# Attention steps of a routed-attention and mixture-of-experts kernel, handed to the engines in another order

## The chip, the cores and the metric

The kernel runs on one core of a Trainium2 chip. The metric is the device time of one execution in microseconds (us). The kernel before took 677.1, 678.21 and 678.61 us in three runs, a median of 678.21.

The core has five instruction streams that matter here. PE (TensorE) does matrix products and transposes. DVE (VectorE), ACT (ScalarE) and POOL (GpSimd) work on whole tiles, and SP (SyncE) issues the DMAs. Each engine takes its own instructions strictly in the order in which they were written; between engines they wait for each other's results.

## What is computed

First comes an attention in which a query sees a key only if both have the same nearest centroid. Then every token goes to one of eight experts by a greedy pass over all logits, and each expert is two matrix products.

```python
q_assign = np.argmax(np.einsum('bhsd,hcd->bhsc', q_n, c_n), axis=-1)
k_assign = np.argmax(np.einsum('bhsd,hcd->bhsc', k_n, c_n), axis=-1)
mask = q_assign[:, :, :, None] == k_assign[:, :, None, :]
scores = scale * np.matmul(q, k.transpose(0, 1, 3, 2))
scores = np.where(mask, scores, -1000000000.0)
attn = np.exp(scores - np.max(scores, axis=-1, keepdims=True))
attn = attn / (np.sum(attn, axis=-1, keepdims=True) + 1e-09)
x = np.matmul(attn, v)                  # heads side by side: (3072, 512)
order = np.argsort(-(x @ w_gate).flatten())
# in that order: a token takes expert e if it has none yet and e has fewer than 384
h = np.maximum(x[mask] @ w1[e], 0.0)
out[mask] = h @ w2[e]
```

Shapes: 4 batches, 8 heads, 768 positions, 64 wide, 16 centroids for each head; 3072 tokens, 512 wide, 8 experts with 1024 hidden columns. All inputs are float32.

## The kernel before

**Tiling.** The attention is cut into 8 units u, each one batch and four heads. A unit has 24 key tiles of 128 keys, and each of them is a step s. float32 operands are split into a high and a low float16 part, which are multiplied separately.

**The steps.** One named step is one closure, mostly one instruction, or a few on one engine. Those that matter here, with their lines:

- `load` (L497) fetches q, k or v through SP's DMA queue, for unit 0 head by head (`load,0,k,2`). `loadc` (L518) fetches the centroids.
- `c0` (L528, DVE), `c1` (L531, ACT, a square root) and `c2` (L536, ten small DVE instructions) normalise the centroids; `c3` (L556, PE) transposes them and `c4` (L559, DVE) copies the result out.
- `split_sc` and `split_hi` (L648, L652, ACT or DVE) scale an operand and write its high part, `split_lo` (L657 on DVE, L659 on POOL) its low part. `dup` (L664, L666, ACT) copies the high part into a second operand.
- `ident` makes the identity matrix on POOL (two instructions in a library file, masks.py), which every PE transpose reads. `misc`, `wtio`, `zqb` and `zkb` are constant fills on POOL.
- `pt` (L746) transposes on PE, `ptc` (L750 on ACT, L752 on DVE) copies the transpose out. `trans` (L740) transposes by DMA instead, for units 1 to 7.
- `cent` and `cent0` (L671, PE) score against the centroids. `hot` and `hh` (L693 to L709) turn the scores into marks for the mask.
- `m_mm` (L788, PE) and `m_rd` (L792, DVE) find a bound of each row's scores. `row0`, `row1` (L806, L810, POOL), `rowt` and `row2` (L813, L817, DMAs from SP's queue) put these bounds into the query operand.
- `b_mm` (L827, L831, PE) makes the scores of a step, `b_exp` (L834, ACT) their exponentials, `res` (L842, POOL or DVE) the low part of these, `av` (L853 to L859, PE) multiplies with v.
- `et` (L571, ACT) is one tiny exponential without use of its own. It makes ACT load the table with the exponential there.
- `out0`, `out1`, `out2`, `hi0`, `hi1` (L863 to L889) divide by the row sums and split; `lg0`, `lg1`, `lg2` (L921 to L935) form the routing logits. For the last unit, `xpt` (L907, PE) and `xpc` (L750, L752) transpose on the core.
- `bb` and `bq` (L1045 to L1066, DVE) begin the routing. `bb,0,i` works on the first three batches, `bb,1,i` on the last; i=0 to 4 (L1045 to L1053) end in the one-hot matrix `oh`, i=5, 6, 8 and 10 (L1055 to L1059, L1066) make integer keys, and i=9 or `bq,x` (L1063) compares with digit offsets.
- `tab` is one of 86 small constants for the routing, nearly all on POOL.

**The order.** The whole attention is a text, `ATT_ORDER`, of 2004 such steps, under `tc.manual_schedule()`. A loop (L1082) reads it word by word and calls the closure of each; so the place of a word in the text sets where its instructions stand in the queues of their engines. The same text has the loads and the DMA transposes in it. After it a second text, `FFN_ORDER`, does the same for routing and experts; its first steps (`pkc`, `cnt`, `sat`, L1175, L1214, L1243) count digits with `oh`.

**The buffers.** Three PSUM banks hold score tiles (`psc`, "sc"), one the centroid scores and logits (`pmx`, "mx"), one the output (`av`). The exponentials lie in a ring of four pairs of steps.

Of the kernel before, what the change touches and what calls it, by code (L numbers as in the profile page):

```python
# [26 lines left out]
hh4,0,k zqb split_sc,0,k,3 load,0,v,- split_hi,0,k,1,P split_lo,0,k,1,P pt,0,ka,1 ptc,0,ka,1,D pt,0,qa,3 ptc,0,qa,3,D
pt,0,qa,2 split_hi,0,k,3,P split_lo,0,k,3,P split_hi,0,k,2,P pt,0,ka,3 split_sc,0,v,- split_hi,0,v,-,P zkb ptc,0,qa,2,D
hh5,0,k pt,0,kb,0 ptc,0,ka,3,D ptc,0,kb,0,D cent0,1,k cent0,1,q hh0,1 hh1,1 dup,0,q,0 hh5,0,q dup,0,k,3 pt,0,qb,0
split_lo,0,k,2,P pt,0,ka,2 hh2,1 dup,0,q,1 hh3,1 hh4,1,q dup,0,k,2 hh4,1,k ptc,0,qb,0,A m_mm,0,3 m_rd,0,3 m_mm,0,4  # L30
split_lo,0,v,-,P m_rd,0,4 ptc,0,ka,2,A m_mm,0,5 m_rd,0,5 hh5,1,q dup,0,k,1 load,1,v,- split_sc,1,v,- vs,0 vh2,0 vact,0 vl2,0
load,1,k,- split_sc,1,k,- tab,0 m_mm,0,2 m_rd,0,2 cent0,2,k cent0,2,q hh0,2 hh1,2 tab,31 hh2,2 pt,0,qb,1 ptc,0,qb,1,D
hh5,1,k tab,3 tab,2 hh3,2 hh4,2,k pt,0,kb,1 split_hi,1,k,-,P hh4,2,q zqm split_lo,1,k,-,P m_mm,0,0 m_rd,0,0 m_mm,0,1
m_rd,0,1 ptc,0,kb,1,A dup,0,q,3 hh5,2,k tab,30 dup,0,q,2 m_mm,0,7 load,1,q,- m_rd,0,7 split_sc,1,q,- pt,0,kb,2 ptc,0,kb,2,D
m_mm,0,11 m_rd,0,11 cent0,3,k cent0,3,q hh0,3 row1,0,0 row0,0,0 load,2,k,- pt,0,qm,0 hh5,2,q split_hi,1,q,-,P ptc,0,qm,0,A
trans,1,ka,- pt,0,qb,2 ptc,0,qb,2,A wd hh1,3 m_mm,0,8 m_rd,0,8 hh2,3 m_mm,0,6 m_rd,0,6 hh3,3 hh4,3,k et split_lo,1,q,-,P
trans,1,qa,- b_mm,0,1 b_exp,0,1 res,0,1,P b_mm,0,0 b_exp,0,0 res,0,0,P hh4,3,q hh5,3,k hh5,3,q m_mm,0,15 m_rd,0,15 m_mm,0,10
m_rd,0,10 m_mm,0,13 m_rd,0,13 tab,32 pt,0,kb,3 cent,1,k,0 cent,1,k,2 cent,1,k,1 ptc,0,kb,3,D split_hi,1,v,-,P
split_lo,1,v,-,P cent,1,k,3 hot0,1,k hot1,1,k load,2,q,- hot2,1,k hot3,1,k tab,7 pt,0,qb,3 ptc,0,qb,3,A b_mm,0,4 b_exp,0,4
tab,5 b_mm,0,3 m_mm,0,9 b_exp,0,3 res,0,4,P m_rd,0,9 row0,0,1 b_mm,0,5 b_exp,0,5 row1,0,1 hot4,1,k hot5,1,k m_mm,0,17  # L40
b_mm,0,2 b_exp,0,2 m_mm,0,16 res,0,2,P dup,1,k,- trans,1,kb,- m_rd,0,17 cent,1,q,0 split_hi,2,k,-,D m_rd,0,16 m_mm,0,20
m_rd,0,20 cent,1,q,3 cent,1,q,2 cent,1,q,1 hot0,1,q hot1,1,q pt,0,qm,1 ptc,0,qm,1,A m_mm,0,12 res,0,3,P m_rd,0,12 hot2,1,q
m_mm,0,14 res,0,5,P m_rd,0,14 av,0,0 av,0,1 av,0,2 dup,1,q,- row0,0,2 row1,0,2 b_mm,0,9 b_exp,0,9 hot3,1,q hot4,1,q hot5,1,q
trans,1,qb,- m_mm,0,19 m_rd,0,19 av,0,3 av,0,4 m_mm,0,22 m_rd,0,22 split_lo,2,k,-,D trans,2,ka,- load,2,v,- b_mm,0,10
b_exp,0,10 b_mm,0,7 b_exp,0,7 b_mm,0,6 b_exp,0,6 res,0,6,P m_mm,0,18 m_rd,0,18 av,0,5 out0,0,0 out1,0,0 out2,0,0,D tab,16
b_mm,0,8 b_exp,0,8 res,0,8,P pt,0,qm,2 m_mm,0,23 m_rd,0,23 ptc,0,qm,2,A hi0,0,0 hi1,0,0 vs,1 m_mm,0,21 b_mm,0,11 dup,2,k,-
# [1492 lines left out]
```

## Time and profile before

| | us |
|---|---|
| median of three runs | 678.21 (677.1 to 678.61) |
| the profiled execution, its own time | 678.19 |
| its span from the first to the last instruction | 676.4 |
| busy in it: PE | 637.9 |
| busy in it: POOL | 512.9 |
| busy in it: DVE | 498.5 |
| busy in it: ACT | 421.3 |

The attention fills the time up to about 371 us, the first routing round lies between there and about 400, and the experts with later routing rounds fill the rest. A busy share over the whole span is an average over these three. In a timeline a row gives the start, the busy time, the engine, the line, what is written and read, and in brackets how long the engine had been idle before, and what it waited for. PE's records overlap their successors, so that a busy PE is not a PE at its full rate. PEclk is the granted clock of TensorE as a share of 2.4 GHz: 1.00 is the higher of its two levels, 0.50 the lower one, 1.2 GHz.

### The profile page before, as it was taken

How to read it: one execution, taken by the hardware profiler on the slowest of the kernel's cores; microseconds unless marked ns; L12 is line 12 of the kernel's file. 1: busy time of each engine (PE TensorE's matmuls, PEld its weight loads, DVE VectorE, ACT ScalarE, POOL GpSimd, SP SyncE). 2: the span in 40 equal slices, each digit the busy share in tenths (PEclk: the TensorE clock that was granted, in tenths of full speed). 3: DMA queues.
4: the chain of work that ended last, by engine and by line, in shares of the span. 5: the costliest groups of instructions: out<-in, count | busy, mean ns of one | idle time of the engine just before them, and what ended most of it. 6: DMA issues, size and time to landing. Idle time of an engine off the chain costs nothing. (4 is left out here: it accounts for less than half of the span.)

```text
span 676.4 us, 19511 instructions
## 1 busy us (share of the span) xinstructions
PE 637.9 (94%) x8154; PEld 428.9 (63%) x8154; DVE 498.5 (74%) x1096; ACT 421.3 (62%) x560; POOL 512.9 (76%) x452
## 2 busy tenths in 40 slices
PE   4899999999999999999988479999999999999996
PEld 4567767777777777777767359554545454545453
DVE  5899999999988989986867777776858585832020
ACT  8987686766767575655554045859484757598221
POOL 8578889899999997999995055858594949498601
PEclk9799999999999999999999669999999999999998
DMA  7668978799959874933123063739576666696101
GB/s 239 140 144 199 210 156 214 144 149 206 207 115 177 196 143 100 167 73 74 29 51 72 25 234 108 267 105 286 182 209 226 179 222 168 240 302 206 47 1 47
DMA packets 175451, 105.85 MB, mean 156 GB/s; under 512 B 135426, under 2 KB 160002, under 8 KB 175362
## 3 DMA queue, kind: packets, MB, share of 16 engines
q1 hardware_dynamic: 171522, 92.01, 56.3%
q0 software_dynamic: 3840, 12.59, 5.0%
q8 instruction: 64, 1.05, 0.7%
q14 instruction: 25, 0.20, 0.1%
HBM read 58.77 MB, written 12.58 MB: 105 GB/s over the span
## 5 line engine op out<-in xcount | busy, mean ns | idle before, releaser
L842 POOL TENSOR_TENSOR rt<-pt 128x768 f16<-128x768 f32 x180 | 276.5, 1558 | 26.6 <-ACT pt L834 25.8
L834 ACT ACTIVATE pt<-sc 128x768 f32<-128x768 f32 x192 | 149.8, 811 | 93.9 <-PE sc L831 73.5
L792 DVE TENSOR_REDUCE mxs<-sc 128x1 f32<-128x768 f32 x192 | 176.1, 951 | 17.7 <-PE sc L788 17.2
L1457 PE MATMUL pf<-xgt,w1h 128*128 128x384 f16 (+1 forms) x640 | 130.2, 295 | 0.3 <-DVE xgt L752 0.2
L856 PE MATMUL av<-vh,rt 128*128 128x65 f16 x1152 | 120.6, 193 | 1.7 <-POOL rt L842 1.6
L853 PE MATMUL av<-vh,pt 128*128 128x65 f16 x1152 | 120.7, 194 | 1.1 <-DVE xb L889 1.1
L855 PE MATMUL av<-vl,pt 128*128 128x64 f16 x1152 | 120.4, 191 | 0.0
L855 PEld LDWEIGHTS <-pt 128*128 128x128 bf16 x1152 | 105.8, 98 | 8.6 <-issue 1.5
L853 PEld LDWEIGHTS <-pt 128*128 128x128 bf16 x1152 | 106.2, 97 | 7.3
L856 PEld LDWEIGHTS <-rt 128*128 128x128 f16 x1152 | 105.3, 97 | 1.9 <-POOL rt L842 1.9
L827 PE MATMUL sc<-qbt,kbt 99*128 99x384 f16 x384 | 94.4, 327 | 1.3 <-DVE mxs L792 0.7
L831 PE MATMUL sc<-qat,kat 128*128 128x384 f16 x384 | 94.4, 327 | 0.0
L788 PE MATMUL sc<-kbt,qbt 80*128 80x384 f16 x384 | 90.5, 330 | 2.2 <-DVE qbt L752 0.5
L1457 PE MATMUL pf<-xgt,w1l 128*128 128x384 f16 (+1 forms) x320 | 89.9, 295 | 0.0
L1415 ACT ACTIVATE wr<-wr 128x1024 f32<-128x1024 f32 x64 | 66.7, 1046 | 25.9 <-DMA wr<-in_moe_w_dram 25.3
L1457 PEld LDWEIGHTS <-w1h 128*128 128x128 f16 x640 | 58.0, 98 | 28.3 <-issue 0.9
L1499 PE MATMUL pf<-w2h,hh 128*128 128x512 f16 (+2 forms) x200 | 73.6, 370 | 0.0
L1499 PE MATMUL pf<-w2l,hh 128*128 128x512 f16 (+2 forms) x200 | 73.6, 370 | 0.0
L1499 PE MATMUL pf<-w2h,hl 128*128 128x512 f16 (+2 forms) x200 | 73.2, 370 | 0.0
L1425 POOL TENSOR_TENSOR w2l<-wr,w2h 128x1024 f16<-128x1024 f32 x32 | 67.6, 2133 | 7.3 <-ACT w2h L1418 6.8
L1425 POOL TENSOR_TENSOR w1l<-wr,w1h 128x1024 f16<-128x1024 f32 x32 | 67.4, 2133 | 1.5 <-ACT w1h L1418 1.3
L1489 DVE SCALAR_TENSOR_TENSOR hl<-pf,hh 128x384 f16<-128x384 f32 x56 | 30.9, 553 | 45.7 <-ACT hh L1486 40.2
(244 smaller groups left out, 1118.3 us busy)
## 6 DMA issues: line engine op xcount, KB each, us to landing
wr<-in_moe_w_dram SPq DMA_DIRECT2D x64, 512.0 KB
...
xg<-xrow,idx POOLq DMA_INDIRECT x24, 6.5
```

The costliest lines, as they stand in the source:

```text
L788: nc.tensor.matmul(p[:, half, :S // 2], QBT[u][:D + C, i, :], KBT[u][:D + C, h * J + half * 3:h * J + half * 3 + 3, :], start=True, stop=True)
L792: nc.vector.tensor_reduce(mxs[u % 3][:, i:i + 1], MP.pop((u, i))[:, :, :S // 2], axis=AX.XY, op=OP.max)
L827: nc.tensor.matmul(ps[:, half, :S // 2], KBT[u][:ER + 3, s, :], QBT[u][:ER + 3, cs, :], start=True, stop=False)
L831: nc.tensor.matmul(ps[:, half, :S // 2], KAT[u][:, s, :], QAT[u][:, cs, :], start=False, stop=True)
L834: nc.scalar.activation(pts[(u * 12 + s // 2) % RP][:, s % 2], MP.pop((u, "b", s))[:, :, :S // 2], AF.Exp, scale=ESC)
L842: (nc.vector if e == "D" else nc.gpsimd).tensor_sub(rts[x][:, s % 2], p.rearrange("p a b -> p (a b)"), hi_view(pts[x])[:, s % 2])
L853: nc.tensor.matmul(o[:, j, :D + 1], hi[:, js], VH[u][:, s, :D + 1], start=(kt == 0 and j == 0), stop=False, skip_group_check=True)
L855: nc.tensor.matmul(o[:, j, :D], hi[:, js], VL[u][:, s, :], start=False, stop=False, skip_group_check=True)
L856: nc.tensor.matmul(o[:, j, :D + 1], r[:, js], VH[u][:, s, :D + 1], start=False, stop=(kt == J - 1), skip_group_check=True)
L1425: nc.gpsimd.tensor_sub(lo, wrs[c], hi)
L1457: nc.tensor.matmul(o, (w1l if i == 2 else w1h)[x][:, c, fs], xgt[x][:, h + int(i == 1), ts], start=(first and i == 0), stop=(last and i == ...
L1499: nc.tensor.matmul(PS["o", p, g], (hl if i == 2 else hh)[x][:, f, g * P:(g + 1) * P], (w2l if i == 1 else w2h)[x][:, f, ds], start=(f == 0 ...
```

## The change

Only the text `ATT_ORDER` changes. It holds the same 2004 steps with the same arguments as before, permuted; nearly every place in it is another one. No closure, no buffer and no size changes, nor does `FFN_ORDER`. The first and the last lines of the text:

```diff
@@ first lines of ATT_ORDER @@
-misc wtio loadc c0 ident c1 c2,0 load,0,k,0 split_sc,0,k,0 c2,1 c2,2 c2,3 c2,4 c2,5 c2,6 split_hi,0,k,0,P load,0,q,0
-split_sc,0,q,0 split_hi,0,q,0,P split_lo,0,q,0,P pt,0,qa,0 c2,7 c2,8 c2,9 load,0,q,2 split_sc,0,q,2 split_hi,0,q,2,P c2,10
+load,0,k,0 split_sc,0,k,0 split_hi,0,k,0,P zkb wtio load,0,q,0 misc split_sc,0,q,0 wd load,0,q,1 loadc split_sc,0,q,1
+load,0,q,2 c0 load,0,k,2 c1 c2,0 c2,1 split_hi,0,q,0,P dup,0,q,0 c2,2 c2,3 c2,4 c2,5 c2,6 split_lo,0,k,0,P c2,7 c2,8 c2,9
+c2,10 load,0,q,3 load,0,k,1 split_sc,0,q,2 split_hi,0,q,2,P et split_lo,0,q,2,P ident pt,0,ka,0 ptc,0,ka,0,D
...
@@ last lines of ATT_ORDER @@
-hi1,7,3,1 bb,0,2 bb,0,3 xpt,0,0 xpt,0,1 xpc,0,A,0 xpt,1,0 xpt,1,1 xpc,0,A,1 xpc,1,D,0 xpc,1,D,1 lg0,7,1,0 lg0,7,1,1 bb,0,4
-tab,81 tab,82 tab,68 tab,71 lg1,7,1 lg2,7,1 xst,7,0 xst,7,1 bb,1,0 bb,1,9 bb,1,1 bb,1,2 bb,1,3 bb,1,4 bb,1,5 bb,1,6 bb,1,8
-bb,1,10 tab,18 tab,19 tab,58 tab,84 tab,63 tab,21 tab,53 tab,66
+out2,7,3,D,1 hi0,7,3,0 xpt,0,0 bb,0,6 hi0,7,3,1 xpt,0,1 xpc,0,A,0 lg1,7,0 lg2,7,0 hi1,7,3,0 xpt,1,0 hi1,7,3,1 xst,7,1 bq,1
+xpt,1,1 xpc,1,D,0 lg0,7,1,0 xpc,1,D,1 bq,2 xpc,0,A,1 lg0,7,1,1 lg1,7,1 bb,0,10 lg2,7,1 bb,1,0 bb,0,8 bb,1,1 bb,1,5 bb,1,9
+bb,1,2 bb,1,6 bb,1,3 bb,1,8 bb,1,10 bb,1,4 tab,42
```

ACT's queue from its start, before. `ss` is the centroids' sum of squares, `ld` a loaded operand, `ka` and `qa` the split operands of unit 0:

```order
L531 ACT_TABLE_LOAD
L531 ACTIVATE ss<-ss 128x1
L648 ACTIVATE ld_76<-ld_76 128x384
L652 ACTIVATE ka<-ld_76 128x6x64
L648 ACTIVATE ld_77<-ld_77 128x384
L652 ACTIVATE qa<-ld_77 128x6x64
```

And further down in ACT's queue before, its 42nd to 46th row (`pt` are exponentials, `etl` the output of `et`):

```order
L750 ACTIVATE qbt_119<-sc 3x768
L750 ACTIVATE qbt_119<-sc 128x768
L571 ACT_TABLE_LOAD
L571 ACTIVATE etl<-ss 128x1
L834 ACTIVATE pt_128<-sc 128x768 x2
```

ACT's queue from its start, after the change:

```order
L648 ACT_TABLE_LOAD
L648 ACTIVATE ld_76<-ld_76 128x384
L652 ACTIVATE ka<-ld_76 128x6x64
L648 ACTIVATE ld_77<-ld_77 128x384 x2
L531 ACT_TABLE_LOAD
L531 ACTIVATE ss<-ss 128x1
L652 ACTIVATE qa<-ld_77 128x6x64
L664 ACTIVATE qb<-qa 128x6x64
L648 ACTIVATE ld_77<-ld_77 128x384
L652 ACTIVATE qa<-ld_77 128x6x64
L571 ACT_TABLE_LOAD
L571 ACTIVATE etl<-ss 128x1
```

The square root stands behind the first splits, and a table load of its own stands before it. The load for the exponential stands at the eleventh place, where it stood before at the 44th. ACT has three table loads where it had two.

POOL's queue around the identity, before (`vm` and `rest` are fills, `wt` a count):

```order
L598 TENSOR_SCALAR vm_127<-vm_127,rest 2x4x2
L574 IOTA wt 128x384
masks.py:197 MEMSET ident 128x128
masks.py:199 AFFINE_SELECT ident<-ident 128x128
L659 TENSOR_TENSOR qa<-ld_77,qa 128x6x64
L659 TENSOR_TENSOR ka<-ld_76,ka 128x6x64
```

And after the change:

```order
L598 TENSOR_SCALAR vm_127<-vm_127,rest 2x4x2
L659 TENSOR_TENSOR ka<-ld_76,ka 128x6x64
L659 TENSOR_TENSOR qa<-ld_77,qa 128x6x64
masks.py:197 MEMSET ident 128x128
masks.py:199 AFFINE_SELECT ident<-ident 128x128
L659 TENSOR_TENSOR qa<-ld_77,qa 128x6x64 x2
```

The identity stands behind two of the subtractions that need ACT's splits (k of head 0 and q of head 2); it stood ahead of all of them.

DVE's queue at the end of the attention, before, from the last `hi1` on:

```order
L889 TENSOR_TENSOR xb_146<-av,xb_146 128x3x64 x2
L1049 TENSOR_TENSOR eq_100<-eq_100,wt_173 128x144
L1051 TENSOR_REDUCE m_101<-eq_100 128x18
L752 COPY xt_150<-sc 128x3x128 x2
L1053 TENSOR_TENSOR oh_102<-eq_100,m_101 128x144
L928 TENSOR_REDUCE mx<-mx 128x48
L935 SCALAR_TENSOR_TENSOR L<-mx,L 128x48
L1045 TENSOR_REDUCE bt_99<-L 128x6
L1063 TENSOR_TENSOR qa<-bt_99,offz_159 128x768
```

After the change, from the same place:

```order
L889 TENSOR_TENSOR xb_146<-av,xb_146 128x3x64 x2
L1063 TENSOR_TENSOR qa<-bt_99,offz_159 128x768
L752 COPY xt_150<-sc 128x3x128 x2
L1063 TENSOR_TENSOR qa<-bt_99,offz_159 128x768
L928 TENSOR_REDUCE mx<-mx 128x48
L1066 TENSOR_SCALAR lo_104<-ku_105 128x18
L935 SCALAR_TENSOR_TENSOR L<-mx,L 128x48
L1045 TENSOR_REDUCE bt_99<-L 128x6
L1059 TENSOR_SCALAR hs_103<-ku_105 128x18
L1047 TENSOR_TENSOR eq_100<-L,bt_99 128x48
L1055 TENSOR_SCALAR msk<-bt_99 128x6
L1063 TENSOR_TENSOR qa<-bt_99,offz_159 128x768
```

Two of the comparisons `bq` now stand between the last output and the last logits, and the key steps (L1055 to L1066) stand in front of `oh`, which comes six rows after the last one shown; before, they stood behind it.

## Rows read from the trace of the kernel before

**Rows 1.** The page: busy us, share of the span, instructions.

```profile
PE 637.9 (94%) x8154; PEld 428.9 (63%) x8154; DVE 498.5 (74%) x1096; ACT 421.3 (62%) x560; POOL 512.9 (76%) x452
```

**Rows 2.** Windows: start:end, length, busy PE PEld DVE ACT POOL, PEclk, DMA share, GB/s.

```profile
0.00:40.00 40.00, 28.71 (x310) 20.09 (x311) 29.42 (x68) 34.73 (x56) 30.64 (x49) 0.87 0.74 195
24.00:34.00 10.00, 9.36 (x62) 5.30 (x62) 8.45 (x17) 9.11 (x13) 7.05 (x6) 0.50 0.58 89
40.00:340.00 300.00, 296.55 (x5093) 223.66 (x5092) 273.97 (x411) 198.73 (x261) 276.14 (x258) 1.00 0.73 148
340.00:370.60 30.60, 27.68 (x568) 21.85 (x565) 22.39 (x35) 16.33 (x24) 23.14 (x33) 1.00 0.32 67
```

**Rows 3.** Timeline of ACT in the first 33 us: start, busy, what, idle before.

```profile
0.76 1.28 ACT L531 ACT_TABLE_LOAD   x1 [0.76 <-PEq L1525]
...
3.75 0.52 ACT L648 ACTIVATE ld<-ld 128x384 f32<-128x384 f32 x1 [0.79 <-DMA ld<-in_k_dram]
...
5.97 0.52 ACT L648 ACTIVATE ld<-ld 128x384 f32<-128x384 f32 x1 [0.17 <-DMA ld<-in_q_dram]
...
30.97 1.28 ACT L571 ACT_TABLE_LOAD   x1
32.27 0.20 ACT L571 ACTIVATE etl<-ss 128x1 f32<-128x1 f32 x1
```

**Rows 4.** Timeline of SP's queue in the first 2 us.

```profile
1.22 0.42 SPq L497 DMA_DIRECT2D ld<-in_k_dram  x1
```

**Rows 5.** Timeline of POOL in the first 15 us.

```profile
5.17 0.29 POOL masks.py:199 TENSOR_SCALAR_AFFINE_SELECT ident<-ident 128x128 f16<-128x128 f16 x1
5.88 0.91 POOL L659 TENSOR_TENSOR qa<-ld,qa 128x384 f16<-128x384 f32 x1 [0.42 <-ACT qa L652]
...
13.07 1.06 POOL L581 MEMSET kb<- 128x1152 f16 x1
```

**Rows 6.** Timeline of DVE in the first 35 us.

```profile
8.58 0.56 DVE L752 COPY kat<-sc 128x768 f16<-128x768 f16 x1 [2.98 <-PE sc L746]
...
10.68 0.36 DVE L693 TENSOR_REDUCE cmx<-mx 128x12 f32<-128x192 f32 x1 [0.88 <-PE mx L671]
...
18.67 1.82 DVE L792 TENSOR_REDUCE mxs<-sc 128x1 f32<-128x768 f32 x2
...
31.01 0.96 DVE L792 TENSOR_REDUCE mxs<-sc 128x1 f32<-128x768 f32 x1 [1.20 <-PE sc L788]
```

**Rows 7.** Timeline of PE: start of the program, drain, and routing.

```profile
6.85 0.82 PE L746 MATMUL sc<-ident,qa 128*128 128x128 f16 x6 [6.85 <-POOL qa L659]
...
31.41 0.84 PE L827 MATMUL sc<-qbt,kbt 99*128 99x384 f16 x2
...
346.73 0.20 PE L856 MATMUL av<-vh,rt 128*128 128x65 f16 x1 [1.56 <-POOL rt L842]
...
377.21 0.30 PE L1214 MATMUL pc<-oh,qa 128*128 128x8 bf16 x6 [2.10 <-DVE oh L1053]
```

**Rows 8.** Timeline of DVE from the last output to the first digit.

```profile
372.54 0.62 DVE L889 TENSOR_TENSOR xb<-av,xb 128x192 f16<-128x192 f32 x2 [0.47 <-ACT xb L885]
...
373.60 0.62 DVE L752 COPY xt<-sc 128x384 f16<-128x384 f16 x2
...
374.60 0.27 DVE L928 TENSOR_REDUCE mx<-mx 128x48 f32<-128x96 f32 x1 [0.16 <-PE mx L922]
...
375.38 0.96 DVE L1063 TENSOR_TENSOR qa<-bt,offz 128x768 bf16<-128x768 f32 x1
...
376.95 0.21 DVE L1053 TENSOR_TENSOR oh<-eq,m 128x48 bf16<-128x48 bf16 x1
...
378.07 0.17 DVE L1243 TENSOR_SCALAR_CACHE_REDUCE scr<-pc 128x8 bf16<-128x8 f32 x1
```

**Rows 9.** SP's queue around the row bounds of unit 1.

```profile
75.49 1.32 SPq L813 DMA_TRANSPOSE mt<-m  x1
...
79.31 0.94 SPq L817 DMA_DIRECT2D qbt<-mt  x1
```

More of the change, by code (lines that the diff above doesn't have):

```diff
@@ L27 @@
[L27 to L46, printed above, removed]
@@ new lines @@
+split_hi,3,q,-,D split_lo,3,k,-,D load,3,v,- rowt,1,0 hi1,0,2 m_mm,1,14 m_rd,1,14 cent,2,q,0 cent,2,q,2 b_exp,0,23
+split_hi,2,v,-,D m_mm,1,15 cent,2,q,1 cent,2,q,3 hot0,2,q hot1,2,q hot2,2,q av,0,18 av,0,19 res,0,20,P m_rd,1,15 row2,1,0
+b_mm,1,2 trans,2,kb,- b_exp,1,2 hot3,2,q res,0,22,P av,0,20 av,0,21 av,0,22 m_mm,1,23 b_mm,1,1 b_mm,1,6 hot4,2,q hot5,2,q
+res,0,23,P av,0,23 m_rd,1,23 split_lo,2,v,-,D res,1,2,P out0,0,3 out1,0,3 m_mm,1,22 m_rd,1,22 b_exp,1,1 res,1,1,P b_exp,1,6
+out2,0,3,D b_mm,1,0 m_mm,1,17 m_rd,1,17 b_exp,1,0 hi0,0,3 hi1,0,3 trans,2,qb,- xtr,0,1 vs,2 vact,2 b_mm,1,3 res,1,0,P
@@ new lines @@
+m_mm,3,0 m_rd,3,0 m_mm,3,1 m_rd,3,1 res,2,1,P av,2,1 m_mm,3,10 m_rd,3,10 m_mm,3,6 m_rd,3,6 res,2,2,P av,2,2 av,2,3 dup,4,k,-
+split_hi,5,k,-,D m_mm,3,2 b_mm,2,11 m_rd,3,2 b_exp,2,11 b_mm,2,10 b_exp,2,10 split_lo,4,v,-,D res,2,4,P res,2,6,P av,2,4
+m_mm,3,12 m_rd,3,12 b_mm,2,8 vl2,3 b_exp,2,8 tab,70 rowt,2,1 row2,2,1 b_mm,2,12 res,2,5,P res,2,11,P av,2,5 out0,2,0
+out1,2,0 out2,2,0,D m_mm,3,9 m_rd,3,9 b_mm,2,9 b_exp,2,12 cent,4,k,0 hi0,2,0 cent,4,k,3 hi1,2,0 res,2,7,P cent,4,k,1
+load,5,v,- cent,4,k,2 hot0,4,k trans,4,qa,- hot1,4,k xtr,1,1 hot2,4,k b_mm,2,13 hot3,4,k hot4,4,k m_mm,3,13 m_rd,3,13
@@ new lines @@
+split_hi,5,v,-,D b_exp,3,11 b_mm,3,10 b_exp,3,9 res,3,9,P m_mm,4,7 m_rd,4,7 av,3,4 m_mm,4,13 xtr,2,1 b_exp,3,10 m_rd,4,13
+av,3,5 out0,3,0 hot5,5,k b_mm,3,8 lg0,2,1 b_exp,3,8 out1,3,0 out2,3,0,D hi0,3,0 m_mm,4,1 m_rd,4,1 rowt,3,1 row2,3,1
+res,3,10,P hi1,3,0 b_mm,3,13 lg1,2,1 b_exp,3,13 b_mm,3,12 b_exp,3,12 lg2,2,1 b_mm,3,14 av,3,6 split_lo,6,k,-,D res,3,8,P
+load,7,q,- m_mm,4,10 av,3,7 m_mm,4,4 m_rd,4,10 m_rd,4,4 av,3,8 b_exp,3,14 res,3,14,P av,3,9 m_mm,4,11 m_rd,4,11 res,3,11,P
+m_mm,4,8 m_rd,4,8 b_mm,3,15 res,3,12,P b_exp,3,15 res,3,15,P av,3,10 b_mm,3,18 b_exp,3,18 res,3,18,P m_mm,4,3 m_rd,4,3
@@ new lines @@
+row1,4,0 av,3,11 out0,3,1 out1,3,1 out2,3,1,D hi0,3,1 hi1,3,1 b_mm,3,16 b_exp,3,16 cent,5,q,0 cent,5,q,1 trans,5,kb,-
+m_mm,4,12 m_rd,4,12 tab,36 b_mm,3,19 cent,5,q,3 cent,5,q,2 hot0,5,q m_mm,4,21 m_rd,4,21 xtr,3,0 hot1,5,q hot2,5,q row0,4,0
+rowt,4,0 av,3,12 row2,4,0 res,3,13,P b_exp,3,19 b_mm,3,20 b_exp,3,20 split_lo,5,v,-,D res,3,16,P hot3,5,q b_mm,3,17
+b_exp,3,17 av,3,13 res,3,17,P res,3,19,P b_mm,3,21 av,3,14 av,3,15 dup,5,q,- m_mm,4,16 m_rd,4,16 b_exp,3,21 b_mm,3,23
+b_exp,3,23 res,3,21,P load,6,q,- m_mm,4,20 m_rd,4,20 av,3,16 av,3,17 hot4,5,q out0,3,2 b_mm,3,22 hot5,5,q out1,3,2
@@ new lines @@
+m_rd,5,22 res,4,22,P tab,18 m_mm,5,18 tab,53 m_rd,5,18 b_exp,5,1 av,4,19 load,7,v,- m_mm,5,13 m_rd,5,13 b_mm,5,0 res,4,23,P
+b_exp,5,0 res,5,1,P res,5,0,P vl2,6 m_mm,5,20 m_rd,5,20 av,4,20 b_mm,5,4 b_exp,5,4 res,5,4,P b_mm,5,3 b_exp,5,3 tab,15
+av,4,21 m_mm,6,8 m_rd,6,8 m_mm,6,4 b_mm,5,5 b_exp,5,5 res,5,5,P m_rd,6,4 av,4,22 row1,5,1 res,5,3,P row0,5,1 av,4,23
+out0,4,3 out1,4,3 m_mm,6,5 m_rd,6,5 b_mm,5,6 b_exp,5,6 res,5,6,P m_mm,6,1 trans,7,ka,- cent,7,k,0 cent,7,k,3 out2,4,3,D
+m_rd,6,1 hi0,4,3 b_mm,5,2 b_exp,5,2 hi1,4,3 res,5,2,P m_mm,6,0 m_rd,6,0 tab,25 b_mm,5,7 b_exp,5,7 m_mm,6,13 cent,7,k,2
```

262 lines of the change are left out of this document (128 added, 134 removed).

## Prediction

> **What bounds the kernel now.** I read the page first: PE is busy for 94% of the span [rows 1]. An average over the whole kernel doesn't say what an order is worth, so I then read the stretches [rows 2]. From 40 to 340 us PE is busy for 296.55 of 300 us: this is PE's stretch, and what reaches it late leaves it late, since there is next to no idle time in which to catch up. DVE is close behind with 273.97. Before it, from 0 to 40, PE is busy for only 28.71 us, and ACT is the full engine, with 34.73. Behind it, from 340 to 370.6, PE is idle for 2.92 us, and after that a serial chain runs: last output, transposes, logits, one-hot, first count. The change permutes the attention's steps alone; the experts are untouched. So there are four places to price: the start (ACT, POOL), the long stretch (PE), the drain, and the serial chain on DVE.
>
> **The start.** I read the timelines of ACT, POOL, DVE and PE [rows 3 to 7]. Before, POOL has the identity at 5.46 (5.17 and 0.29), then does a low part (start 5.88, 0.91), and PE's first instruction, a transpose, starts at 6.85, when that low part is in [rows 5, 7]. Its first table load ran from 0.76 to 2.04 while ACT had nothing else to do: the first data came at 3.75 [rows 3].
>
> After the change the identity stands behind the low part of q of head 2, and this needs ACT's high part, ten entries down ACT's queue. I walk that queue. The loads of k and q move up by one issue on SP, since the centroids now come behind them; an issue takes 0.42 us [rows 4]. The second piece of q, which came at 5.97 [rows 3], comes at about 5.5. Its scaling, 0.52, ends at 6.0. Then comes a table load that wasn't there, 1.28, to 7.3; the square root, about 0.2 (the other one-column activation took 0.20 [rows 3]), to 7.5; then four pieces of 384 columns at about 0.48 each (a record of 0.52, a little overlapped), to 9.45. POOL then subtracts, 0.91, to 10.35, and builds the identity, some 0.6 (its second half alone is 0.29 [rows 5]), to 11.0. POOL's own fills don't come into it: they grow by the 1.06 of a fill that moved up [rows 5] and are over at about 6. So PE starts at 11.0 instead of 6.85, 4.1 later.
>
> How much of this survives? DVE waited 2.98 us for the first transpose and 0.88 for the first centroid scores [rows 6]. With the same 3.3 us from the first transpose to the start of the marks in the new order, the marks start at 14.3 instead of 10.68, +3.6. Up to the first row maximum, which was at 18.67 [rows 6], ACT stays the pacer, and now has two more table loads ahead of it than in the old order up to there, 2 x 1.28 = 2.56. I put the first row maximum at +3.0, between 2.56 and 3.6. From there one load is given back: the load for the exponential stood at 30.97, in front of the first exponentials [rows 3], and stands there no more. That makes the first scores, at 31.41 [rows 7], about 3.0 - 1.28 = 1.7 late. DVE's share of the lateness is larger, but DVE had a wait of 1.20 us for PE at 31.01 [rows 6], into which some of it goes. I take **+2.0** for the start: between 1.7, by ACT, and 3.0, by DVE, nearer to the first, since PE is the fuller one behind it.
>
> Its bounds come from the clock. In the stretch 24 to 34 the granted clock is 0.50, the lower level, with PE busy for 9.36 of 10 us [rows 2]. Before that stretch PE had waited much, as the sum for 0 to 40 shows; in it PE was full, and after it the level is 1.00 again. If PE's work comes later and denser, this stretch can go: half of 9.36 is 4.7 us of PE's time, but the rest of the chain (ACT, DVE) has to keep up, so I count at most 2 us back. If the lower level lasts instead from the first transpose on, more work falls into it. Range of the start: 0 to +3.5.
>
> At this place the Trainium skill speaks against the change. The two loads in the trace show no more than their 1.28 us: the one at 30.97 ends at 32.25, and the next activation starts at 32.27 [rows 3]. The Trainium skill, "ScalarE: Activation LUTs", section "What ACT_TABLE_LOAD costs", gives about 1283 ns for the load, as here, and a drain of about 1380 ns on top, for each switch of table. By that the load in front of the square root would put the identity at 12.4 instead of 11.0, and the sum below would be 1.4 us higher. The trace doesn't show this drain, and the sum goes by 1.28.
>
> The clock has a page too. "TensorE: Matmul & The Clock Gate" of the Trainium skill, section "What's actually happening", says that "the default state is throttled, and activity releases the throttle". The trace agrees in that the level is 0.50 for a time in the thinly used first 40 us and 1.00 in the full stretch behind it [rows 2]; by the rule a later first transpose means a later release, which is on the side of the loss that I forecast anyway.
>
> **The long stretch.** The same steps are there, with the same distances on the whole: between the scores of a step and its product with v lie about as many instructions as before, and the three score banks turn over at the same pace. I find two places that have become tighter. In unit 1, the first group's row bounds go through a transpose and a copy on SP's queue, issued at 75.49 and 79.31, with 0.94 for the second [rows 9]: 4.8 us from the first issue to the end of the second. In the new order PE has about 4.7 us of its own work between the row step and the first scores of that unit, where it had about 10 (counted in PE instructions at their durations); a stall of 0 to 2 us. In unit 7 the two DMA transposes of k and q stand back to back, 0 to 1 us. On the other side, PE is idle for 300 - 296.55 = 3.45 us in this stretch, which a better order could win back; its records overlap, so that some more idle time doesn't show. I take **0**, with -4 to +4: there is no row that prices 1600 moved steps one by one.
>
> **The drain.** The work left after the last bound (`m_mm`) is about the same, 21 score steps against 23, 30 products each. The one long stall before, 1.56 us at 346.73 for a low part on POOL [rows 7], falls at a place where the new order has the low parts of unit 7 earlier. I take **-0.5**, from -2 to +1; all idle time of PE in the drain is 2.92 [rows 2].
>
> **The serial chain.** I take the last product with v as fixed and follow DVE [rows 8]. The first `bq` moved in between `hi1` (372.54, 0.62 for two) and the copies (373.60) takes 0.96, the time of the same instruction at 375.38; there were 373.60 - 373.16 = 0.44 us of other, now moved, work in its place, so the copies start some 0.4 later. The second `bq`, another 0.96, stands in front of the reduction that started at 374.60, where DVE had waited 0.16: the reduction starts at 375.5, +0.9. From there to `oh` six more small instructions stand in the way, at about 0.18 each (the one-hot took 0.21 [rows 8]), 1.1: `oh` is +2.0 late. PE waits for `oh`: it did so for 2.10 us until 377.21 [rows 7]. But the instructions behind `oh` have become fewer. Before, DVE took from 376.95 to 378.07 to get from `oh` to the first digit, 1.1 us; PE's count itself is over in 0.3. In the new order only two fills stand between, and the digit follows some 0.4 earlier. Net **+1.6**, with +0.8 to +2.0. Nothing hides it: PE, ACT and POOL have no other work there, and the expert weights are loaded only when this round has named an expert.
>
> **The sum.** +2.0 + 0 - 0.5 + 1.6 = +3.1. The profiled execution took 678.19 us, 1.8 around a span of 676.4, and the median of the runs is 678.21; so 678.2 + 3.1 = **681.3**.
>
> **The rivals.**
> - *The waits of PE close up (faster).* Place: PE from 40 to 370.6. Price: up to 3.45 + 2.92 = 6.4 us of idle time [rows 2]. At 4.5 us won it outweighs the 3.1 and the 1.36 of the bound below; with the full 6.4 the time is 681.3 - 6.4 = 674.9. For it: the stall of 1.56 is in one piece and depends on the order alone [rows 7]. Against it: it needs most of the idle time there, and DVE, at 273.97 of 300, has little to give. With the start's clock on its side (-2) it needs only 2.5 us. 676 is its time; 0.25.
> - *The tight places stall (slower still).* Unit 1's row bounds +2, unit 7's transposes +1: 684.3. For it: SP's queue takes 4.8 us for the first [rows 9]. Against it: work of other units stands between. 0.15.
> - *The late start is absorbed.* PE and DVE have enough slack from 18 to 40, with the load at 30.97 gone and the wait of 1.20 used up; the chain costs 1.0 and the drain gives 0.5: 678.7, no change that can be told. 0.14.
> - *A table load costs more than its record.* ACT stands still behind each load; the identity, and all that follows, comes 1.4 later: 682.7. The gap of 0.02 us at 32.27 speaks against it [rows 3]. 0.04. This is what the page of the Trainium skill on ACT would give.
>
> **How the numbers follow.** The forecast itself, 681.3, has 0.42. 0.2% is 1.36 us, which is about what a measurement of this kernel can tell from no change: same is 676.85 to 679.57. Slower: 0.42 + 0.15 + 0.04 = 0.61; same 0.14; faster 0.25. The low end is 675.8, short of the full price of the first rival; the high end is 685.5, the second rival and a start at +3.2. Slower holds most of the chance, with a range of its own from 679.6 to 685.5.
>
> **What would show it.** Right: three table loads on ACT, at about 1, 6 and 9.5 us; PE's first transpose at 10 to 12; the first row maximum at 21 to 22; the first scores at 32 to 34; from the last product with v to the first digit 9.1 us instead of 7.5 (378.07 less 370.6, where the drain's stretch ends). Wrong: a first row maximum before 20, or a PE that is past the same unit boundary earlier than before in spite of its start; `oh` less than 1 us late against the last product; or PE idle for more than 6 us between 40 and 340, which would name the tight places.

## The result, and the profile after

After the change the kernel takes 684.7 us, the median of five runs (682.15 to 687.85), where before took 678.21: a ratio of 1.010 with a 95% interval of 1.006 to 1.014, so 4 to 10 us more. The profiled execution is the longest of the five, 687.85, with a span of 686.1: 9.7 above the one of before. What the rows below add up to is therefore that execution's 9.7, not the median's 6.5. The five runs lie 5.7 us apart, those of before 1.6; what spreads them isn't shown, since only one execution has a profile. One run among the experiments, of 1441.79 us, is in a slow state and is left out of its kernel's median.

The page's busy line, to hold against [rows 1]:

```profile
PE 640.5 (93%) x8154; PEld 431.2 (63%) x8154; DVE 496.2 (72%) x1096; ACT 423.3 (62%) x561; POOL 505.3 (74%) x452
```

The work is the same, but for one ACT instruction more, a table load. The 9.7 us are waiting and clock. The last three stretches of [rows 2], with the ends moved with the work:

```profile
32.00:42.00 10.00, 9.53 (x88) 5.92 (x86) 7.73 (x16) 6.27 (x10) 7.64 (x8) 0.51 0.91 181
40.00:340.00 300.00, 291.62 (x4895) 218.20 (x4893) 267.73 (x399) 195.67 (x256) 265.20 (x255) 0.99 0.77 150
340.00:379.70 39.70, 39.70 (x788) 31.16 (x784) 28.18 (x48) 22.69 (x32) 27.57 (x28) 1.00 0.35 68
```

PE is idle for 8.38 us from 40 to 340, where it was 3.45, and not at all in the drain, where it was 2.92. The granted clock of the long stretch is 0.99, not 1.00.

**The start.** ACT's timeline (start, busy, what, idle before), against [rows 3]:

```profile
0.74 1.28 ACT L648 ACT_TABLE_LOAD   x1 [0.74 <-PEq L1525]
...
5.47 1.28 ACT L531 ACT_TABLE_LOAD   x1
6.76 0.20 ACT L531 ACTIVATE ss<-ss 128x1 f32<-128x1 f32 x1
...
8.91 1.28 ACT L571 ACT_TABLE_LOAD   x1
10.21 0.20 ACT L571 ACTIVATE etl<-ss 128x1 f32<-128x1 f32 x1
...
12.12 0.52 ACT L648 ACTIVATE ld<-ld 128x384 f32<-128x384 f32 x1 [0.47 <-DMA ld<-in_k_dram]
```

Three table loads, and behind the third a wait for a piece of k, which the prediction didn't look for. PE's first transpose, the first marks and the first row maximum on DVE, and the first scores on PE, against [rows 6, 7]:

```profile
10.45 0.80 PE L746 MATMUL sc<-ident,ka 128*128 128x128 f16 x6 [7.16 <-POOL ident masks.py:199]
13.75 0.36 DVE L693 TENSOR_REDUCE cmx<-mx 128x12 f32<-128x192 f32 x1
21.70 2.69 DVE L792 TENSOR_REDUCE mxs<-sc 128x1 f32<-128x768 f32 x3 [0.21 <-PE sc L788]
33.95 0.85 PE L827 MATMUL sc<-qbt,kbt 99*128 99x384 f16 x2
```

They are late by 3.60 (6.85), 3.07 (10.68), 3.03 (18.67) and 2.54 (31.41).

**The long stretch.** The table of waits of PE from 40 to 340 (us in all, times, longest):

```profile
PE mx L921 <- DMA xt<-xb: 2.2, 1, 2.2
PE sc L788 <- ACT pt L834: 1.9, 1, 1.9
PE av L853 <- DVE xb L889: 1.7, 1, 1.7
PE sc L788 <- DMA qbt<-qb: 1.3, 1, 1.3
```

Four single stops. The windows that hold them (at 115, 175, 215 and 300), and the two stretches that follow the first and the third:

```profile
115.00:125.00 10.00, 7.83 (x157) 5.98 (x154) 8.06 (x11) 3.41 (x6) 8.04 (x11) 1.00 1.14 180
126.00:132.00 6.00, 6.00 (x100) 4.32 (x99) 5.46 (x10) 3.82 (x5) 3.73 (x3) 0.72 0.48 92
175.00:182.00 7.00, 5.70 (x127) 4.52 (x125) 5.97 (x8) 5.38 (x6) 4.49 (x4) 1.00 1.23 181
215.00:222.00 7.00, 5.13 (x95) 3.77 (x94) 4.65 (x7) 4.09 (x6) 6.86 (x6) 1.00 1.14 248
222.00:228.00 6.00, 6.00 (x70) 3.73 (x67) 3.69 (x4) 2.65 (x4) 2.94 (x4) 0.72 1.01 305
300.00:308.00 8.00, 6.35 (x82) 4.19 (x79) 7.07 (x8) 4.79 (x8) 7.78 (x5) 1.00 1.03 159
```

The four hold 2.17 + 1.30 + 1.87 + 1.65 = 6.99 of the 8.38 us of idle time. And at two of them more is lost than the stop: soon after it PE is full, but its clock falls to the lower level for some 3.4 us, so that 6 us have a mean of 0.72, which is 6 x 0.28 = 1.7 us of full clock. In the kernel before, the clock is 1.00 all the way from 40 to 370, and no matmul of `b_mm` (384 columns) takes longer than 0.33 us there, where in the falls it takes up to 0.53.

Behind each stop stands a step in another place. SP's queue around the first:

```profile
106.45 6.72 SPq L740 DMA_TRANSPOSE qat<-qa  x1
113.22 0.58 SPq L497 DMA_DIRECT2D ld<-in_q_dram  x1
113.84 0.63 SPq L895 DMA_DIRECT2D xrow<-xb  x1
116.12 5.01 SPq L898 DMA_TRANSPOSE xt<-xb  x1
```

The transposing load of `xtr,1,0` (L898) starts 2.9 us behind the load of q and behind a store, and takes 5.01 us. In the kernel before, the same load of q stood in front of it too, but was issued 6 us earlier, and there was no store between:

```profile
106.91 0.51 SPq L497 DMA_DIRECT2D ld<-in_q_dram  x1
112.96 1.70 SPq L898 DMA_TRANSPOSE xt<-xb  x1
```

So the new order has put the store in front, and the load comes late: the transpose ahead of it takes 6.72 us, right behind a load of v (106.01) that came after that transpose before (which took 3.57, at 101.99). No run moves the load of v alone or the store alone.

For the other three: the DMA transpose that `m_mm,4,0` reads is issued at 173.16 behind a store (`xst,1,1`, at 172.46) that didn't stand there before; the load of q of unit 6 is issued at 213.08 instead of well ahead, and ACT, which has to split it, can't free a score bank meanwhile (the trace names no releaser for ACT's idle time of 2.37 us there); `split_lo` of v of unit 7 takes 4.08 us on DVE in front of an output split. Each of these waits went when its step was moved (all four mended, below).

**The sum of the profiled execution**, up to the last product with v: first scores 2.54, idle time in the long stretch 8.38 - 3.45 = 4.93, clock 2 x 1.7 = 3.4, drain -2.9: 8.0. The first step behind that product, DVE's L863, is 9.14 late, 379.81 against 370.67. The 1.1 that is missing has room between the first scores and 42, where PE still runs at the lower level (0.51 in the stretch 32 to 42; before, that stretch was 24 to 34).

**The serial chain** on DVE, against [rows 8]:

```profile
379.81 0.16 DVE L863 TENSOR_SCALAR rc<-av 128x6 f32<-128x6 f32 x1
...
383.08 0.61 DVE L752 COPY xt<-sc 128x384 f16<-128x384 f16 x2
...
384.47 0.26 DVE L928 TENSOR_REDUCE mx<-mx 128x48 f32<-128x96 f32 x1
...
385.00 0.20 DVE L1045 TENSOR_REDUCE bt<-L 128x6 f32<-128x48 f32 x1
385.12 0.17 DVE L1059 TENSOR_SCALAR hs<-ku 128x18 int32<-128x18 int32 x1
385.24 0.21 DVE L1047 TENSOR_TENSOR eq<-L,bt 128x48 bf16<-128x48 f32 x1
...
386.78 0.20 DVE L1053 TENSOR_TENSOR oh<-eq,m 128x48 bf16<-128x48 bf16 x1
...
387.37 0.17 DVE L1243 TENSOR_SCALAR_CACHE_REDUCE scr<-pc 128x8 bf16<-128x8 f32 x1
```

Four steps of the old chain that each need the one before, the last of them in [rows 8] (L1053 at 376.95), start 0.22 to 0.24 us apart:

```profile
376.26 0.20 DVE L1047 TENSOR_TENSOR eq<-L,bt 128x48 bf16<-128x48 f32 x1
376.49 0.18 DVE L1049 TENSOR_TENSOR eq<-eq,wt 128x48 bf16<-128x48 bf16 x1
376.71 0.20 DVE L1051 TENSOR_REDUCE m<-eq 128x6 bf16<-128x48 bf16 x1
```

From L863 to the first digit it is 387.37 - 379.81 = 7.56 us; before, 378.07 - 370.67 = 7.40. The copies are 0.34 late against L863, the reduction 0.73, `oh` 0.69, and the digit 0.16.

### The profile page after: what moved, and what is told of

Read it like the earlier page. It is cut to its first block, busy times and chain, and to the rows that moved or that the text cites. A ratio compares the mean times of both kernels' runs of the same rounds, so it can differ in the third digit from the quotient of the medians.

```text
span 686.1 us, 19516 instructions
## 1 busy us (share of the span) xinstructions
PE 640.5 (93%) x8154; PEld 431.2 (63%) x8154; DVE 496.2 (72%) x1096; ACT 423.3 (62%) x561; POOL 505.3 (74%) x452
## 5 line engine op out<-in xcount | busy, mean ns | idle before, releaser
L842 POOL TENSOR_TENSOR rt<-pt 128x768 f16<-128x768 f32 x180 | 268.9, 1514 | 38.5 <-ACT pt L834 36.8
L827 PE MATMUL sc<-qbt,kbt 99*128 99x384 f16 x384 | 96.2, 332 | 0.3 <-ACT qbt L750 0.2
L831 PE MATMUL sc<-qat,kat 128*128 128x384 f16 x384 | 96.5, 333 | 0.0
```

The lines of the kernel that those rows point to most:

```text
L827: nc.tensor.matmul(ps[:, half, :S // 2], KBT[u][:ER + 3, s, :], QBT[u][:ER + 3, cs, :], start=True, stop=False)
L831: nc.tensor.matmul(ps[:, half, :S // 2], KAT[u][:, s, :], QAT[u][:, cs, :], start=False, stop=True)
L842: (nc.vector if e == "D" else nc.gpsimd).tensor_sub(rts[x][:, s % 2], p.rearrange("p a b -> p (a b)"), hi_view(pts[x])[:, s % 2])
```

## Experiments

Each was timed in several rounds with the kernel before beside it, and a difference is one against the median of before in the same rounds: 678.41 for the new start, the old start, the new drain and the four mended stops; 679.33 for the new middle, the routing chain, the identity and the square root; 678.83 for the three mended causes, the first stop and the other table load; 679.49 for the piece of k. The text of steps could be cut and joined where no step then comes ahead of one that it needs.

**Which part costs what.** Five kernels take one part of the new order each.

*The new start alone.*

```diff
 ATT_ORDER = the first 182 steps of the new order
-  + the rest of the new order
+  + the rest of the order before
```

> The order before, with only its start (all 181 steps up to the first scores) taken from the new order. Theory 1, places: the start costs its own 3.0 us and no more, since PE's lag in the trace of the new order stays near 3 to 4 us up to 120 us; about 681.2. Theory 2, shift: the late start moves every transfer against the other engines, and the later stalls are its consequences; then most of the whole 6.5 us comes with it, 683 to 685. Neither theory has it under 680.

680.77, a ratio of 1.003 (1.001 to 1.005): +2.4 of the 6.5.

*The old start, all else new.*

```diff
-ATT_ORDER = the new order
+ATT_ORDER = the first 181 steps of the order before + the rest of the new order
```

> The new order, with only its start taken from the order before. Theory 1, places: 3.0 us less than the new order, about 681.7, and PE's four stalls between 120 and 310 us (for the logits' transposed operand, for unit 4's queries, behind the wait for unit 6's load, behind a slow subtraction on DVE) are still there. Theory 2, shift: the stalls go with the late start, 678 to 679.

680.9, 1.003 (1.001 to 1.005): +2.5. The two halves add up to 4.9, which is inside the interval of the whole. The stop for `xtr,1,0` is there again (its load takes 5.15), and the clock falls behind it and once more at 300:

```profile
122.00:128.00 6.00, 6.00 (x108) 4.32 (x107) 5.64 (x11) 3.85 (x5) 3.77 (x3) 0.72 0.49 93
300.00:304.00 4.00, 3.92 (x49) 3.09 (x49) 1.97 (x4) 1.66 (x3) 3.78 (x7) 0.57 0.02 4
```

*The new drain and what follows, behind the old order.*

```diff
 ATT_ORDER = the order before
-  with its last 199 steps
+  with the new order's last 199 steps
```

> The order before, with only the end of the attention (199 steps, from the last row bounds of unit 7 on, with the steps of the routing behind it) taken from the new order. Theory 1, places: PE's lag fell by 3.3 us in the drain of the new order, and the serial chain on DVE behind it was 0.2 us longer; so 678.2 - 3.1, about 675. Rival: the gain in the drain is only a debt that a late PE pays back, since the other engines were ahead of it by then; without a late PE there is none, 678 to 678.5. By the terms of the prediction (drain -0.5, chain +1.6) it would be 679.3.

681.15, 1.004 (1.002 to 1.005): 2.7 slower, not faster. PE waits for a low part on POOL, the very wait of [rows 7], and longer, and the clock falls behind it:

```profile
343.59 0.20 PE L856 MATMUL av<-vh,rt 128*128 128x65 f16 x1 [2.95 <-POOL rt L842]
344.00:348.00 4.00, 4.00 (x23) 2.04 (x19) 2.04 (x5) 1.19 (x2) 4.00 (x4) 0.57 0.01 2
```

So the new drain isn't a better drain. Joined to the old order it finds POOL behind: in the changed kernel's drain POOL is the one that waits, for ACT, up to 3.55 us at a time.

*The new middle alone.*

```diff
 ATT_ORDER = the order before
-  its steps from unit 1 to the drain
+  the new order's steps from unit 1 to the drain
```

> The order before at the start and from the 1807th step on (end of the attention, routing chain); between them the new order. Theory 1: the middle costs something of its own, namely the waits of PE between 115 and 300 us, 3.2 us in the profiled execution of the run with only the old start up to its last unit; then 680.5 to 682 here, and the drain of the new order adds little behind a late middle. Theory 2: the 2.5 us of the run with the old start come from the drain, which alone cost 2.7; then this one is at the order before, 678.4.

684.11, a ratio of 1.0075 (1.005 to 1.010): +4.8, above what either theory gave. With the new drain behind it the middle costs 2.5, with the old one 4.8; the old order with the new drain costs 2.7. PE waits 2.14 us for POOL's low part in this old drain. The two don't add up as parts; that middle and drain hand each other's backlog on is the reading of these waits, not a run of its own.

*The new routing chain alone.*

```diff
 ATT_ORDER = the order before
-  with its last 42 steps
+  with the new order's last 42 steps (from bq,0 on)
```

> The order before, with only the last 42 steps from the new order (behind the last product with v: comparisons and key steps in front of the one-hot). The prediction's step: 1.6 us more, 680.0. What the trace of the new order shows (7.66 us from the last product to the first digit, against 7.50): 0.2 us more, 678.6. Some steps of the first three batches that stood in this chain are out of the way here, so down to 0.3 us less is possible.

678.57 beside 679.33, 1.000 (0.998 to 1.001): the chain costs nothing that can be told, and the 1.6 us of the forecast are outside the interval.

**Why the start is late.** All are built on the new start alone (680.8), but the last.

*The identity first on POOL.*

```diff
+ident load,0,k,0 split_sc,0,k,0 ...
-... split_hi,0,q,2,P et split_lo,0,q,2,P ident pt,0,ka,0
+... split_hi,0,q,2,P et split_lo,0,q,2,P pt,0,ka,0
```

> The order before with the new start, in which the identity is now POOL's first step. Theory of the identity: PE's late first transpose (10.4 us) makes the start late; it would come at 7.0 and most of the 2.4 us of the new start go, 678.5 to 679. Theory of the table loads: ACT's queue sets the time of the first row bounds, and PE's first transposes don't matter: within 0.5 us of the new start, 680.3 to 681.

682.53, the median of eight runs, 1.005 (1.003 to 1.006): no gain. PE's first transpose comes at 7.46, but the next waits for POOL's low part and comes hardly earlier than in the changed kernel, where it came at 11.34:

```profile
11.25 0.82 PE L746 MATMUL sc<-ident,qa 128*128 128x128 f16 x6 [2.97 <-POOL qa L659]
```

*The square root first on ACT, so that the table is loaded twice and not three times.*

```diff
+loadc c0 c1 load,0,k,0 split_sc,0,k,0 ...
-... load,0,q,1 loadc split_sc,0,q,1 load,0,q,2 c0 load,0,k,2 c1 ...
+... load,0,q,1 split_sc,0,q,1 load,0,q,2 load,0,k,2 ...
```

> The order before with the new start, in which the load of the centroids, its sum of squares and the square root stand first, as they did before, so that ACT has one table load less (two, the first of them in its idle time). Theory of the table loads: 1.28 us less than the new start, 679.5. Theory of the identity: the identity still waits for ACT's tenth step, which comes 1.5 us earlier, so the same 1.3 us less or a little more; it is told apart from the other only by the run with the identity first. If neither holds: 680.8.

682.92, 1.004 (1.002 to 1.006): no gain either. ACT had 1.28 us less to do and waited for data instead:

```profile
11.78 0.52 ACT L648 ACTIVATE ld<-ld 128x384 f32<-128x384 f32 x1 [0.71 <-DMA ld<-in_k_dram]
```

*All three named causes mended at once.*

```diff
+loadc c0 c1 ident load,0,k,0 ...
-... load,0,q,1 loadc split_sc,0,q,1 load,0,q,2 c0 load,0,k,2 c1 ...
+... load,0,q,1 split_sc,0,q,1 load,0,q,2 load,0,k,2 ...
-... split_hi,0,q,2,P et split_lo,0,q,2,P ident pt,0,ka,0
+... split_hi,0,q,2,P split_lo,0,q,2,P pt,0,ka,0
-hh4,3,q ... trans,1,qa,- b_mm,0,1
+hh4,3,q ... trans,1,qa,- et b_mm,0,1
```

> The new order's first 182 steps and before's order behind them, as in the run of the new start alone (680.8, +2.4 on before), but with GpSimd's identity put first, the root's steps on the constants put first (so that ScalarE loads a table twice instead of three times), and the exponentials' root of et put back just ahead of the bias product of unit 0 that wants it. Theory that the start is late for these three together: the time comes within 0.8 of before (ratio 0.999 to 1.001). Rival, that what the new start is late for is the order in which its loads arrive and in which ScalarE and GpSimd split them: it stays 2 to 4 above before (ratio 1.003 to 1.006).

686.42, 1.011 (1.009 to 1.012): +7.6, the worst of all starts, and the theory with it is gone. ACT now stands still at the place where it had waited 0.47:

```profile
12.35 0.52 ACT L648 ACTIVATE ld<-ld 128x384 f32<-128x384 f32 x1 [2.56 <-DMA ld<-in_k_dram]
```

That it is slower even than the new start was expected by no theory. One thing that the others don't have is `et`'s table load at 36.14; its share wasn't measured. In the profiled execution, the shortest of the five (684.23, 6.0 over the one of before), 2.9 us are there at the first scores (34.33), 4.6 at DVE's last L863 (375.27), and the other 1.4 come behind the attention, where none of these edits stands. From that L863 to the end the fourteen profiled executions take between 304.6 and 307.2 us, before 305.7 and this one 307.2.

*The piece of k that ACT waits for, ahead of v.* SP's queue of the changed kernel shows why that piece is late: a small piece of k, then v (768 KB), and only then, as the first of the two in the last row, k's last small piece (192 KB):

```profile
4.05 0.43 SPq L497 DMA_DIRECT2D ld<-in_k_dram  x1
4.53 0.43 SPq L497 DMA_DIRECT2D ld<-in_v_dram  x1
5.00 0.98 SPq L497 DMA_DIRECT2D ld<-in_k_dram  x2
```

Before, all four pieces of k were issued ahead of v.

```diff
 (on top of the three mends)
-pt,0,qa,0 load,0,v,- ... hh1,0 load,0,k,3 hh2,0
+pt,0,qa,0 load,0,k,3 load,0,v,- ... hh1,0 hh2,0
-hh4,3,q ... trans,1,qa,- et b_mm,0,1
+hh4,3,q ... trans,1,qa,- b_mm,0,1
-loadc c0 c1 ident
+loadc c0 c1 et ident
```

> The start with three causes mended, with two more steps moved: the load of the last small piece of k of unit 0 (192 KB, on which ScalarE waited 2.56 until 12.35) ahead of the load of v (768 KB), behind which the new order puts it, and the exponentials' root of et right behind the constants' step c1, so that ScalarE has both table loads behind it before its first data. Theory that the start is late for its loads' order: ScalarE's wait before that piece falls below 1, the first row maximum comes before 20 (18.67 before, 21.70 after the change) and the time is 678 to 680 (ratio 0.999 to 1.002). Rival, that it lies in the order of the work behind the loads: the wait goes, the first row maximum stays above 20 and the time 2 or more above before (ratio 1.003 or more).

678.59, 0.9985 (0.9972 to 0.9999): the start's whole cost is gone. ACT, with both table loads done by 4.4, works through without a wait, and the first row maximum comes 3.0 us earlier than in the run before this one (18.60 against 21.63):

```profile
8.66 1.33 ACT L648 ACTIVATE ld<-ld 128x384 f32<-128x384 f32 x3
```

```profile
18.60 2.67 DVE L792 TENSOR_REDUCE mxs<-sc 128x1 f32<-128x768 f32 x3
```

Up to 12.35 the two kernels differ on ACT only in `et`, which makes ACT later here, and in that load; so it is the load's place that kept ACT standing after the three mends. How much of the time itself is due to the load and how much to `et`'s place isn't separated. The clock differs too: from 27 to 39 us its mean is 0.72 here and 0.57 in the run before this one. But the same difference lies between the kernel before (0.57 from 24 to 36) and the next run (0.72 there), whose times are the same. The kernel is 0.9 under before, less than the 0.2% that can be told.

*The other table load, in the kernel before.*

```diff
-... c0 ident c1 c2,0 ...
+... c0 ident c1 et c2,0 ...
-hh4,3,k et split_lo,1,q,-,P
+hh4,3,k split_lo,1,q,-,P
```

> The kernel before with one step moved: the step et right behind the constants' step c1, so that ScalarE loads the exponential's table at about 3 us, while it waits for its first data, and not at 30.97 just ahead of the first bias work. Theory that the table load at 30.97 lies on TensorE's path: 0.8 to 1.3 less (677.1 to 677.6 where before is 678.4, ratio 0.998 to 0.999). Rival, that TensorE has work enough beside it there: no difference (ratio 0.9995 to 1.0005).

678.67 beside 678.83, 1.000 (0.999 to 1.001): the load at 30.97 [rows 3] was hidden all the time.

**The stops of the long stretch.**

*All four mended, in the changed kernel.*

```diff
-load,4,q,- behind m_mm,2,10; xst,0,0 behind m_rd,2,19
+both behind trans,3,kb,-
-load,6,q,- behind res,3,21
+load,6,q,- behind trans,5,kb,-
-split_lo,7,v,- behind av,5,17
+split_lo,7,v,- behind hi1,5,2
-m_mm,4,0 m_rd,4,0 behind m_mm,3,17
+m_mm,4,0 m_rd,4,0 ahead of m_mm,4,5
```

> The new order with four moves, one for each stall of PE over 1.2 us between 100 and 310 us: a load and a store put behind the transposing DMA they stood ahead of (stall 2.2 us), a load put a few dozen steps earlier (2.0 us), DVE's subtraction of v of unit 7 put behind the division that waits for it (1.8 us), the first bound of unit 4 put two score steps later (1.3 us). Theory 1, places: the sum of 7 us in the profiled execution goes; since the runs of the new order differ by up to 5.7 us, which I put down to these waits on transfers, the median should fall from 684.7 to 677 to 680, and the runs should lie within 1.5 us of each other. Rival: the waits only uncover the next ones behind them, as ACT and DVE are nearly as full as PE there: 682 to 685.

686.63, 1.011 (1.008 to 1.014): no gain. The four waits went, and four others came, of 3.2 (for DVE's `xb`), 1.7, 1.4 and 1.0, with three falls of the clock, at 126, 184 and 219. The runs still lie 5.4 us apart, where the first theory wanted 1.5. The stretch of the longest wait:

```profile
126.00:134.00 8.00, 5.59 (x70) 4.42 (x70) 6.06 (x9) 4.49 (x6) 4.32 (x3) 0.57 0.58 160
```

This wait is one that the mend made: the store of `xst,0,0`, now issued at 120.91, holds a buffer of `xb` that ACT wants to write:

```profile
127.28 0.49 ACT L885 ACTIVATE xb<-av 128x384 f16<-128x384 f32 x1 [4.92 <-DMA xrow<-xb]
```

*Only the first stop mended, with the old start, and the store early instead of late.*

```diff
 (on top of the old start with all else new)
-load,4,q,- behind m_mm,2,10; xst,0,0 behind m_rd,2,19
+load,4,q,- behind trans,3,kb,-; xst,0,0 behind xtr,0,0
```

> Before's start and the new order from unit 1 on, as in the run with the old start (680.9, +2.5 on before), with two DMA steps moved: the store of xst,0,0 right behind the transposing load xtr,0,0, and the load of q of unit 4 behind the transposes of unit 3, so that the transposing load on which TensorE stood 2.56 at 118 has no load and no store just ahead of it on SP. Theory that this stop is the middle's cost: 678 to 679 (ratio 0.999 to 1.001). Rival, that the next tight place comes out in its stead: 680 to 682 (ratio 1.002 to 1.005).

679.72, 1.0025 (1.001 to 1.004): +0.9 by the medians and +1.7 by the ratio, where the old start without the mend had +2.5 and +1.9; the two intervals overlap, so no gain is shown. The stop is gone:

```profile
112.34 1.41 SPq L898 DMA_TRANSPOSE xt<-xb  x1
```

```profile
110.00:125.00 15.00, 15.00 (x296) 11.74 (x294) 14.73 (x26) 8.35 (x13) 13.04 (x15) 1.00 0.72 166
```

But PE's idle time from 40 to 340 is 7.16 all the same: it stops elsewhere, for 1.6 at 80, 1.6 at 213 and 1.7 at 298. The stop at 80 is for unit 1's row bounds, the first of the two tight places that the prediction named:

```profile
81.81 0.50 PE L827 MATMUL sc<-qbt,kbt 99*128 99x384 f16 x2 [1.57 <-DMA qbt<-mt]
```

The store of `xst,0,0`, now issued at 68.50, stands in front of their transpose (73.59) and copy, and the copy is issued 6.0 us behind the transpose, where without the mend it was 3.8. The falls of the clock are missing here, though: 1.00 all through, even behind the stop at 298 that was followed by one without the mend. So the rival is right on the idle time, and if the mend gained at all, the clock may be where; that isn't shown.

## Why the prediction was right, and where its steps were not

**The forecast** was 681.3 with a range of 675.8 to 685.5; 684.7 lies inside, on the side that held most of the chance. Its sum of +3.1 is half of the 6.5. That the time still lies inside is in part luck: the long stretch was priced too low by 2.5 us or more and the serial chain too high by 1.6, and these two errors work against each other. Two of its own signs of being wrong came, `oh` less than 1 us late and PE idle for more than 6 us. The terms stand thus.

**The start: +2.0, measured +2.4.** The marks came as the walk down ACT's queue gave them: first transpose 10.45 (11.0 worked out), first marks 13.75 (14.3), first row maximum 21.70 (21.67), table loads at 0.74, 5.47 and 8.91. But the reason was only half the reason. The prediction gave the lateness to ACT's two more loads and to the identity behind a low part; taking the identity or one load away brought nothing, and taking away all three together made it worse. There is a second limit at the same place, the piece of k behind v on SP's queue: ACT's wait for it grows from 0.47 to 0.71 and 2.56 us as ACT gets there earlier. Of the clock, whose bounds were 2 us back or more lost, nothing came: the stretch at the lower level has the same mean over 12 us in both profiles, 0.57 (24 to 36 before, 30 to 42 after), only later. The step that failed here is the sentence that the loads of k and q "move up by one issue": it is true of the first pieces, and the last piece of k moved behind 768 KB. The step on the load at 30.97, "one load is given back", failed too: that load cost before nothing, so nothing came back, and the first scores are 2.54 late and not 1.7.

On the table load itself the row decided rightly. The load at 5.47 ends at 6.75 and the next activation starts at 6.76; the one at 8.91 ends at 10.19, the next starts at 10.21. The Trainium skill, "ScalarE: Activation LUTs", section "What ACT_TABLE_LOAD costs", gives about 1283 ns for the load, as here, and some 1380 ns of drain on top; the drain isn't seen in this trace either.

**The long stretch: 0, with -4 to +4.** This is the term that was mis-sized. In place of it stand 4.93 us of idle time and 3.4 of clock in the profiled execution, and +2.5 to +4.8 in the timed kernels that have the new middle and the old start. The places named, unit 1's row bounds and unit 7's transposes, are not among the four stops; the first of them stalls for 1.57 us only when a mend puts a store in front of it. What was overlooked is, at three of the four, a step that nobody waits for at once (a store, a load, DVE's subtraction of v) in front of one that somebody waits for, and at the other one, at 220, a load that was itself issued too late. And the prediction counted a stop at its own length, where two of four cost 1.7 us more through the clock. It did name the sign to look for, "PE idle for more than 6 us between 40 and 340", but not these places.

**The drain: -0.5, from -2 to +1.** In the changed kernel all 2.92 us of idle time are gone there. But the new drain behind the old order is 2.7 slower, with the same wait on POOL. The step failed in form: this drain has no price of its own. PE comes there later in the new order, and POOL is ahead of it.

**The serial chain: +1.6, measured 0.** The copies are 0.34 late (0.4 worked out) and the reduction 0.73 (0.9), but `oh` is 0.69 late and not 2.0, and the digit 0.16. The step that failed is the price of "six more small instructions", "at about 0.18 each". In the old chain (L1047 to L1053) each of DVE's small steps needs the one before, and starts some 0.23 us behind it. The key steps don't need the step just ahead of them: L1059 starts 0.12 behind L1045, and L1047, which needs L1045, 0.12 behind L1059, thus at the same 0.24 as if nothing stood between. They lie in gaps that were there. Behind `oh` the chain is then shorter, as the prediction said. The chain alone gave 1.000.

**The rivals.** That the waits close up is refuted by 8.38 us of idle time. That tight places stall has the right sign and, by luck, nearly the right time, 684.3: the stalls are at other places. That the late start is absorbed is refuted by +2.4, and that a load costs more than its record by the gap of 0.02.

**What stays open:** why the three mended causes cost 7.6, of which the trace shows 4.6 in the attention; whether the piece of k ahead of v would do alone, without the three mends, which no run tried; and whether the first mend of the long stretch gained by the clock. When a stop becomes a fall of the clock isn't settled either. Its length doesn't decide: a stop of 0.83 us at 119 (the new middle alone) is followed by a fall, and the stop of 1.66 at DVE's `xb` is in one run (the old start, at 300) and not in another (the first stop mended, at 298).
